# Output projection's weights loaded head group by head group, with a new recorded order, in a fused attention and MLP block

## The chip, the cores and the metric

The kernel runs on one core of one Trainium2 chip. The metric is device time in microseconds (us), the median of the runs; the kernel before was run three times. Beside these there is one profiled execution, of which every engine's instructions, the DMA queues and the semaphores are recorded. A core has five instruction streams: TensorE (PE for matmuls, PEld for the loads of their stationary operand), VectorE (DVE), ScalarE (ACT), GpSimd (POOL) and SyncE (SP), which here issues all DMAs. Each stream runs strictly in the order in which it was written.

## The reference

Inputs are bf16: 2048 rows of 576 numbers, 32 heads of 18, an MLP of 4608. Cut to what matters:

```python
def _A_ref(x, wq, wk, wv, wo, beta):          # x: layernorm of the input
    q, k, v = split_heads(x @ wq), split_heads(x @ wk), split_heads(x @ wv)
    ...
    for s in range(4):                        # four segments of 512 rows
        logits = einsum('bhqd,bhkd->bhqk', qs, ks) * scale + mask
        a_dot = einsum('bhqk,bhkd->bhqd', softmax(logits), vs)
        a_mem = (phi(qs) @ M) / (phi(qs) @ z + 1e-06)
        outs.append(g * a_mem + (1.0 - g) * a_dot)
        M, z = M + phi(ks).T @ vs, z + phi(ks).sum()
    return merge_heads(outs) @ wo
def _B_ref(x, w1, b1, w2, b2):
    return gelu(x @ w1 + b1) @ w2 + b2
h = x + _A_ref(layernorm(x), ...)
return h + _B_ref(layernorm(h), ...)
```

## The kernel before

**Tiling.** The 2048 rows are 16 tiles `t` of 128 rows, in 8 chunks `c` of 256. The steps of a tile have names, which the text uses:

- `x_p` (line 262) loads a tile of x; `bnp`, `aggrp`, `powp`, `nmrp`, `applyp`, `againp` (lines 363 to 383) are its layernorm; `PTx` (393) turns it on PE, with the copy `PTcx` (396) to SBUF, or `Tx` (154) turns it with a transposing DMA.
- `proj` (351, 355) multiplies with wq, wk, wv. The last 64 of the 576 rows of the weights are done for two products side by side in half the array each (`prest`, 427), or, for those listed in the table `WHOLE`, with a full-height matmul of their own. `pev` (482 to 491) takes the result from PSUM to SBUF. `PTq`, `PTk` (507) with `PTcq`, `PTck` (510, 511), or the transposing DMAs `Tq`, `Tk` (154), turn queries and keys into QT and KT.
- `score` (599): 16 small matmuls into one PSUM tile of four banks, `exp` (603) on ACT, `mask` (607) on POOL, `value` (615) back on PE. There are 80 such visits, and all use the same four banks: `score` v+1 cannot start before `exp` v is done. Two to four visits make one group of heads; `f_T`, `f_rec`, `f_gate`, `f_mul` (630 to 642) divide and gate the sum.
- The memory of earlier segments: `k_exp`, `k_relu`, `k_min`, `k_add`, `MZ`, `MZadd`, `MZblk` (520 to 549), and for the queries `m_exp` to `m_mul` and `mem` (561 to 577). The gate is made once by `g_exp`, `g_add`, `g_rec`, `g_omg`, `g_gmz` (337 to 345).
- `oT` (650) turns the attention's output, `wo` (659) multiplies with the output projection's weights, `res` (662) adds x, `bnb` to `againb` (675 to 695) are the second layernorm.
- `F1q` and `F1` (351, 355, with `rest`, 726, for the last 64 rows of w1) are the first layer of the MLP, `F1e` (745 on ACT, 747 on DVE) adds the bias, `gelu` (768) runs on ACT, `F2` (828) is the second layer, `ot` (834) adds the residual, which comes back from DRAM by `hc` (819).

**Order.** The functions only record operations with what they read and write. What runs, and where, is in five tables written out by hand of a search: `ORDER` (line 874) lists the operations as they are issued, one list for all engines; `FLIP` names those that go to their other engine (ACT instead of DVE, DVE instead of POOL, and so on); `WHOLE` is named above; `PLACE` gives each PSUM result its bank. Banks 0 to 3 are free for any use; banks 4 to 7 are the tile of the scores, or four more single banks (`st` in the profile) while no scores are in them. So a PSUM bank that is written anew waits for whoever still reads it.

**DMAs.** SP issues all of them in the order of `ORDER`. Eight semaphores are handed out in turn, so an issue also waits until the DMA eight issues before it has landed. A waiting issue holds back everything behind it.

**Output weights.** `wo_t` (128 partitions x 5 blocks x 576) holds the 576 rows of wo rearranged: partition 32i+p of block b has row 144i+32b+p, for the four groups i of 144 rows (8 heads each). Block 4 has 16 rows per group.

**Warm-up.** 37 matmuls on zeros (`zeros`, 334) stand between the first real PE work; they need `pq`, which the memset `pq0` (293) clears.

Of the kernel before, what the change touches and what calls it, by code (L numbers as in the profile page):

```python
# [16 lines left out]
def kernel(  # L17
# [15 lines left out]
    nc = tc.nc  # L33
    P = 128
    x = A_x.flatten_outer_dims()
    of = out.flatten_outer_dims()
    S, D = x.shape
# [8 lines left out]
    KT = 5  # L46
    HALF = D // 2
    G = H // 4
    R = D // 4
# [15 lines left out]
    def sbuf(name, shape, dt=BF16):  # L65
# [29 lines left out]
    }  # L95
    FLIP = {
# [8 lines left out]
    }  # L105
    WHOLE = {
        204, 397, 407, 417, 424, 487, 488, 561, 645, 792, 870, 871, 1103, 1519, 1840, 2159, 2160,
# [40 lines left out]
    def dma(name, kb, desc, issue, rd=(), wr=(), after=()):  # L148
        o = op(name, "SP", issue, rd, wr, after=after)
        o.kb, o.desc = kb, desc  # L150
        return o
# [7 lines left out]
    wo_t = sbuf("wo_t", [KT, D])  # L159
# [119 lines left out]
    rows_of = A_wo.rearrange("(i r) n -> i r n", r=R)  # L279

    def last_wo():
        nc.sync.dma_start(out=wo_t[0:96, 4, :], in_=A_wo[P:P + 3 * R, :].rearrange("(i r) n -> i r n", r=R)[:, 0:32, :])
        nc.sync.dma_start(out=wo_t[96:112, 4, :], in_=A_wo[D - 16:D, :])

    memset("wo0", "POOL", wo_t[96:P, 4, :], 0.0, [("wo", 4)])
    for b in range(4):
        kb = 180 if b < 3 else 144
        dma(("wo", b), kb, kb // 18, lambda b=b: nc.sync.dma_start(out=wo_t[:, b, :], in_=rows_of[:, 32 * b:32 * b + 32, :]), (), [("wo", b)])
    dma(("wo", 4), 18, 1, last_wo, (), [("wo", 4)])
# [565 lines left out]
    for c in range(NCH):  # L855
# [193 lines left out]
```

## Time and profile before

| | |
|---|---|
| three runs, us | 459.26, 459.88, 460.39; median 459.88 |
| the profiled execution's own time | 461.19 us |
| its span, from the first to the last instruction | 459.5 us |
| busy in the span: DVE, ACT, POOL | 270.4 us (59%), 327.1 us (71%), 232.6 us (51%) |
| read from HBM, written | 60.09 MB, 7.08 MB |
| mean granted TensorE clock | 0.996 of full speed |

A line of the profile's timeline has the start, the busy time, engine, source line, operation, `out<-in`, shapes and count; in square brackets is the engine's idle time before it and what ended it. "PEclk" is the share of the full TensorE clock that was granted. Busy time of PE counts a matmul until its modelled end, and consecutive ones overlap. "issue" means that an engine stood still although the profile shows nothing that it waited for. The lines themselves are shown in the prediction, where they are used.

### The profile page before, as it was taken

Reading aid. Unit: us, or ns where it says so; the run is one execution under the profiler, and the core shown is the slowest. Engines: PE = TensorE matmul, PEld = TensorE weight load, DVE = VectorE, ACT = ScalarE, POOL = GpSimd, SP = SyncE. Lnnn points to the kernel's source line nnn. Section 1 sums busy time; section 2 is a strip of 40 time slices with the busy share of each in tenths; the row PEclk is TensorE's granted clock in tenths of the full one; section 3 lists DMA queues with packets and bytes.
Section 4 is the critical chain, followed back from the end, with each engine's and each line's share of the span. In section 5 each row is a group of like instructions: output and inputs, shape, how many; then the busy total and the mean of one; then the engine's idle time right before and its main releaser. Section 6 shows DMA issues by size and latency. Waiting matters only on the chain.

```text
span 459.5 us, 14513 instructions
## 1 busy us (share of the span) xinstructions
PE 448.6 (98%) x6110; PEld 335.6 (73%) x6110; DVE 270.4 (59%) x616; ACT 327.1 (71%) x317; POOL 232.6 (51%) x419
## 2 busy tenths in 40 slices
PE   8899989999999999999999999999999999999997
PEld 6555868677667777766777767777777888888886
DVE  6697978878676676686757586752425432112221
ACT  5688879988878897878778879798967155453430
POOL 7677858687976557756462697654025002000000
PEclk9899999999999999999999999999999999999999
DMA  8589988554569675879545885676558647655212
GB/s 233 148 220 258 250 158 235 185 129 102 147 167 225 162 173 161 211 165 203 145 126 163 190 200 127 183 218 186 147 156 189 195 123 198 205 175 172 88 41 66
DMA packets 113253, 78.42 MB, mean 171 GB/s; under 512 B 47731, under 2 KB 111139, under 8 KB 113187
## 3 DMA queue, kind: packets, MB, share of 16 engines
q1 hardware_dynamic: 113187, 77.48, 65.3%
q8 instruction: 48, 0.79, 0.8%
q14 instruction: 18, 0.15, 0.1%
HBM read 60.09 MB, written 7.08 MB: 146 GB/s over the span
## 4 chain that ended last, share of the span: by engine, by line
PE 87%; DMA 5%; SPq 2%; issue 1%; DVE 1%; ACT 1%; POOL 1%; ACTq 0%; DVEq 0%
PE bank L351 27%; PE bank L828 24%; PE st L351 9%; PE st L828 6%; PE st L599 5%; PE bank L615 4%; PE bank L659 3%; PE bank L726 3%; PE bank L355 2%; DMA xT<-xn 1%; PE bank L569 1%; DMA x_p<-in_A_x_dram 1%; DMA x_b<-in_A_x_dram 1%; DMA w1g<-in_B_w_dram 1%; PE st L726 1%
## 5 line engine op out<-in xcount | busy, mean ns | idle before, releaser
L603 ACT ACTIVATE pt<-st 128x2048 bf16<-128x2048 f32 x80 | 150.1, 1877 | 43.8 <-PE st L599 34.2
L828 PEld LDWEIGHTS <-hT 128*128 128x128 bf16 x1188 | 111.4, 98 | 28.0 <-issue 1.2
L828 PE MATMUL bank<-w_sb,hT 128*128 128x288 bf16 (+1 forms) x936 | 131.3, 284 | 0.0
L607 POOL TENSOR_SCALAR_AFFINE_SELECT pt<-pt 128x512 bf16<-128x512 bf16 x128 | 80.0, 641 | 42.7 <-ACT pt L603 40.9
L351 PEld LDWEIGHTS <-w1g 128*128 128x128 bf16 x944 | 86.5, 98 | 18.4 <-issue 7.2
L351 PE MATMUL bank<-xn2T,w1g 128*128 128x256 bf16 (+1 forms) x760 | 93.7, 269 | 0.0
L747 DVE TENSOR_TENSOR hT<-bank,b1T 128x512 bf16<-128x512 f32 x77 | 52.0, 684 | 66.8 <-PE bank L351 63.0
L768 ACT ACTIVATE hT<-hT 128x1536 bf16<-128x1536 bf16 (+4 forms) x25 | 66.2, 2662 | 6.2 <-DVE hT L747 5.9
L745 ACT ACTIVATE hT<-bank,b1T 128x256 bf16<-128x256 f32 x66 | 27.5, 472 | 33.2 <-PE bank L351 32.9
L351 PE MATMUL bank<-wqkv,xT 128*128 128x432 bf16 (+1 forms) x208 | 45.4, 348 | 1.9 <-DVE QT L510 1.9
L351 PEld LDWEIGHTS <-xT 128*128 128x128 bf16 x264 | 24.4, 99 | 20.3 <-issue 4.9
L599 PE MATMUL st<-QT,KT 32*128 32x128 bf16 x1280 | 32.8, 218 | 2.4 <-issue 2.4
L834 DVE TENSOR_TENSOR ot<-bank,hc 128x288 bf16<-128x288 f32 (+1 forms) x26 | 11.6, 447 | 38.6 <-PE bank L828 25.6
L828 PE MATMUL st<-w_sb,hT 128*128 128x288 bf16 (+1 forms) x252 | 34.1, 277 | 0.0
L599 PEld LDWEIGHTS <-KT 32*128 32x128 bf16 x1280 | 18.7, 93 | 18.8 <-issue 16.0
L630 DVE STREAM_TRANSPOSE bank<-bank 128x512 f32<-128x512 f32 x32 | 23.2, 724 | 9.0 <-PE bank L615 8.7
L564 POOL TENSOR_TENSOR pq<-ek,pq 128x512 bf16<-128x512 bf16 x24 | 27.7, 1154 | 1.4 <-DVE ek L563 1.1
L351 PE MATMUL st<-xn2T,w1g 128*128 128x256 bf16 x184 | 24.7, 273 | 0.0
L643 POOL TENSOR_TENSOR o_nat<-t,t 128x288 bf16<-128x288 f32 x24 | 19.4, 808 | 9.7 <-DVE t L642 6.9
L667 POOL TENSOR_TENSOR h_t<-h_t,b_bc 128x576 f32<-128x576 f32 x16 | 20.6, 1284 | 6.6 <-DVE xn L685 6.6
L615 PE MATMUL bank<-pt,v_aug 128*19 128x128 bf16 x1280 | 23.6, 220 | 0.0
L615 PEld LDWEIGHTS <-v_aug 128*19 128x19 bf16 x1280 | 17.9, 92 | 5.7 <-issue 3.7
(159 smaller groups left out, 639.7 us busy)
## 6 DMA issues: line engine op xcount, KB each, us to landing
w1g<-in_B_w_dram SPq DMA_DIRECT2D x57, 512.0 KB, 4.2
w_sb<-in_B_w_dram SPq DMA_DIRECT2D x12, 432.0 KB, 5.5
wqkv<-in_B_w_dram SPq DMA_DIRECT2D x10, 512.0 KB, 4.6
hd<-h_t SPq DMA_DIRECT2D x16, 288.0 KB, 3.7
hc<-hd SPq DMA_DIRECT2D x32, 144.0 KB, 3.7
w1g<-in_B_w_dram SPq DMA_DIRECT2D x114, 32.0 KB, 3.2
x_b<-in_A_x_dram SPq DMA_DIRECT2D x18, 144.0 KB, 4.1
hT<-in_B_w_dram SPq DMA_DIRECT2D x5, 512.0 KB
```

The costliest lines, as they stand in the source:

```text
L351: nc.tensor.matmul(out=acc, lhsT=lhsT_of(slice(0, P), k), rhs=rhs_of(slice(0, P), k), start=start and k == 0, stop=False, skip_group_check ...
L564: op(("m_add", n), "POOL", lambda: nc.gpsimd.tensor_tensor(out=pq[:], in0=e_g, in1=pq[:], op=ALU.add), ["ek"], ["pq"])
L599: nc.tensor.matmul(out=st4[:, i, n * P:(n + 1) * P], lhsT=KTs[(2 * s0 + kt) % NK][rows, g, :], rhs=QTs[(2 * c + qt) % NQ][rows, g, :], sta ...
L603: op(("exp", v), "ACT", lambda pt=pt: nc.scalar.activation(out=pt[:], in_=open_four("scores")[:], func=ACT.Exp, scale=scale), [st], [("pt" ...
L607: op(("mask", v), "POOL", lambda n=n, pt=pt: nc.gpsimd.affine_select(out=pt[:, :, n * P:(n + 1) * P], in_=pt[:, :, n * P:(n + 1) * P], pat ...
L615: nc.tensor.matmul(out=bank(ox)[32 * i:32 * i + E, (g % 4) * P:(g % 4) * P + P], lhsT=v_augs[(2 * s0 + kt) % NV][:, G * i + g, :], rhs=pt[ ...
L630: op(("f_T", n), "DVE", lambda: nc.vector.transpose(out=bank(ox), in_=bank(ox)), [], [ox])
L667: op(("hb", t), "POOL", lambda: nc.gpsimd.tensor_tensor(out=h_t[:], in0=h_t[:], in1=b2_bc[:], op=ALU.add), ["b2"], hk)
L745: nc.scalar.activation(out=dst[:, j, :], in_=acc()[:, j, :], func=ACT.Identity, bias=b1T[:, j0 + j:j0 + j + 1], scale=1.0)
L747: op(name, "DVE", lambda: nc.vector.tensor_tensor(out=dst, in0=acc(), in1=bias, op=ALU.add), [tok, "b1T"], keys, alt=("ACT", by_act), afte ...
L768: op(("gelu", c, f0, f), "ACT", lambda: nc.scalar.activation(out=hT[:, f0:f, :], in_=hT[:, f0:f, :], func=ACT.Gelu_apprx_tanh), [], [("hT" ...
L828: nc.tensor.matmul(out=bank(b)[:, 0:w], lhsT=hT[:, q, tl * P:(tl + 1) * P], rhs=w2_sb[:, q, hs], start=(q == 0), stop=(q == NF - 1))
```

## The change

The load of wo is cut the other way. Before, block b was one DMA over all four groups: source rows as (4 groups) x (32 rows) x 576, 128 partitions; block 4 took a DMA for three groups (3 x 32 x 576) and one for the last 16 rows, six DMAs in all. After, group i is one DMA: source as (32 rows) x (5 blocks, 4 for the last group) x 576, into its 32 partitions, and one for the last 16 rows, five DMAs. The bytes are the same to within the rows of block 4 (for groups 0 to 2, block 4 takes 32 rows in both).

All five tables are new. The operations, their number and what they compute are the same. By the new tables:

- `WHOLE` has 16 entries instead of 17: the pair `rest` of chunk 1's first F1 products is now done in halves, three `prest` entries changed places;
- from DVE to ACT: 8 more `applyp` and 2 more `applyb`; from ACT to DVE: 6 `pev` and 2 `PTcx`; between DVE and POOL, 2 `againb` and 1 `againp` go to DVE, and some memsets change engine;
- DVE begins with the memset of MZacc ahead of `pq0` (before: `pq0` first);
- in the list of SP, `x_p` of tile 5 is the 16th DMA, and the loads of wo come right behind it (before: the three loads of blocks 1 and 4 come ahead of it, with that of b1 between); the first load of w2 stands 45th (before: 19th), the first of w1 21st (before: 29th);
- `Tk` of tile 4 is issued after score 8 (before: after score 14), `Tk` of tile 3 after score 7 (before: 11), `Tx` of tile 5 after score 5 (before: 6);
- `b1Tc` has `MZadd`, `MZadd`, `pev` ahead of it on DVE (before: `k_min`, `g_omg`, `g_omg`, `pev`, `aggrp`).

```diff
     PLACE = {
-        0: 0, 1: 1, 2: 2, 3: 3, 4: 0, 5: 4, 6: 3, 7: 1, 8: 4, 9: 0, 10: 2, 11: 0, 12: 5, 13: 2, 14: 2, 15: 1, 16: 4,
...
+        0: 0, 1: 1, 2: 2, 3: 3, 4: 3, 5: 2, 6: 3, 7: 3, 8: 5, 9: 2, 10: 0, 11: 5, 12: 4, 13: 1, 14: 4, 15: 3, 16: 6,
...
-    rows_of = A_wo.rearrange("(i r) n -> i r n", r=R)
-
-    def last_wo():
-        nc.sync.dma_start(out=wo_t[0:96, 4, :], in_=A_wo[P:P + 3 * R, :].rearrange("(i r) n -> i r n", r=R)[:, 0:32, :])
-        nc.sync.dma_start(out=wo_t[96:112, 4, :], in_=A_wo[D - 16:D, :])
-
     memset("wo0", "POOL", wo_t[96:P, 4, :], 0.0, [("wo", 4)])
-    for b in range(4):
-        kb = 180 if b < 3 else 144
-        dma(("wo", b), kb, kb // 18, lambda b=b: nc.sync.dma_start(out=wo_t[:, b, :], in_=rows_of[:, 32 * b:32 * b + 32, :]), (), [("wo", b)])
-    dma(("wo", 4), 18, 1, last_wo, (), [("wo", 4)])
+
+    for i in range(4):
+        n = KT if i < 3 else 4
+        rows = A_wo[i * R:i * R + 32 * n, :].rearrange("(b r) n -> r b n", r=32)
+        dma(("wo", i), 36 * n, 2 * n, lambda i=i, n=n, rows=rows: nc.sync.dma_start(out=wo_t[32 * i:32 * i + 32, 0:n, :], in_=rows), (), [("wo", i)])
+    dma(("wo", 4), 18, 1, lambda: nc.sync.dma_start(out=wo_t[96:112, 4, :], in_=A_wo[D - 16:D, :]), (), [("wo", 4)])
...
     ORDER = [
-        21, 64, 35, 53, 37, 27, 65, 55, 0, 66, 41, 67, 1, 68, 69, 70, 56, 57, 26, 10, 71, 72, 31, 51, 73, 22, 74, 75,
...
+        22, 55, 21, 20, 65, 49, 0, 53, 10, 1, 54, 56, 23, 66, 30, 2, 67, 57, 36, 68, 69, 70, 58, 5, 3, 71, 28, 143,
...
```

More of the change, by code (lines that the diff above doesn't have):

```diff
@@ L68 @@
     PLACE = {
[26 rows of a table removed]
[26 rows of a table added]
     }
     FLIP = {
[8 rows of a table removed]
[7 rows of a table added]
     }
     WHOLE = {
-        204, 397, 407, 417, 424, 487, 488, 561, 645, 792, 870, 871, 1103, 1519, 1840, 2159, 2160,
+        264, 397, 407, 417, 424, 487, 488, 561, 792, 793, 871, 1103, 1104, 1519, 2159, 2160,
     }
```

337 rows, old and new, of tables (FLIP, ORDER, PLACE) are left out of this document.

## The prediction

> **What bounds the kernel now.** I read the page first, then the sums by stretch, PE's waits, and the chain of the first 75 us.
>
> ```profile
> span 459.5 us, 14513 instructions
> ...
> PE 448.6 (98%) x6110; PEld 335.6 (73%) x6110; DVE 270.4 (59%) x616; ACT 327.1 (71%) x317; POOL 232.6 (51%) x419
> ...
> q8 instruction: 48, 0.79, 0.8%
> ```
>
> PE is busy 98% of the span. So the time is PE's own work plus the stretches in which it stands still or runs slowly.
>
> ```profile
> 14.61:18.02 3.41, 1.52 (x26) 0.83 (x15) 1.09 (x3) 2.43 (x3) 3.10 (x8) 1.00 0.50 152
> 18.02:21.44 3.42, 3.40 (x30) 1.94 (x30) 3.17 (x7) 0.77 (x2) 2.05 (x5) 0.50 0.51 126
> ...
> 60.00:70.00 10.00, 7.96 (x177) 6.76 (x174) 7.55 (x18) 7.13 (x6) 5.76 (x9) 1.00 0.76 136
> 70.00:260.00 190.00, 190.00 (x2834) 137.24 (x2832) 136.84 (x309) 159.81 (x139) 126.79 (x215) 1.00 0.67 170
> ...
> 270.00:350.00 80.00, 80.00 (x1126) 61.03 (x1127) 41.41 (x95) 65.54 (x60) 39.39 (x69) 1.00 0.66 171
> ...
> 360.00:450.00 90.00, 90.00 (x804) 73.31 (x802) 23.08 (x44) 35.72 (x50) 3.74 (x6) 1.00 0.50 147
> ```
>
> Columns: stretch and length, busy time (count) of PE, PEld, DVE, ACT, POOL, granted clock, DMA share, GB/s. From 70 to 450 us PE is full in all but two short stretches; nothing can be won there except by less work. The losses lie before 70 us: standing still, and one stretch of 3.42 us at half clock right behind a stretch in which PE was busy only 1.52 of 3.41.
>
> ```profile
> PE st L599 <- issue: 2.4, 2, 2.0
> PE bank L351 <- DVE QT L510: 1.9, 1, 1.9
> PE bank L334 <- DVE pq L293: 1.2, 1, 1.2
> PE bank L427 <- DMA xT<-xn: 1.1, 1, 1.1
> PE bank L427 <- DVE b1T L847: 0.9, 1, 0.9
> PE bank L726 <- DVE ot L834: 0.3, 1, 0.3
> PE bank L726 <- DMA w1g<-in_B_w_dram: 0.2, 1, 0.2
> ```
>
> These are all of PE's waits: 8.0 us, 1.2 of them the start. With the half clock (3.4 us for 1.7 us of work) 9.7 us are not full-speed work, and 8.0 of those lie between 15 and 64 us. That is the most that an order with the same work can win there.
>
> **PE's work does not change.** Operations and counts are the same but for `WHOLE`: one `rest` fewer there, so two matmuls of 256 columns less.
>
> ```profile
> 263.98 0.87 PE bank L351 x8
> ...
> 52.95 0.22 PE L355 MATMUL bank<-xn2T,w1g 128*128 128x128 bf16 x1
> 53.10 0.40 PE L599 MATMUL st<-QT,KT 32*128 32x128 bf16 x16
> ```
>
> Eight such matmuls take 0.87 us, so two give 0.2 us back. What an order could change besides is the switching between full-height matmuls and those in parts of the array: a score begins 0.15 us after the matmul of 128 columns ahead of it, which by the first row's rate (0.109 for 256) needs 0.055, so a switch costs about 0.1 us. Counted along PE's list there are 265 switches in both orders: no difference. ACT's changes between exp and gelu are also 22 in both. So everything hangs on the waits.
>
> **The wait at 16 us and the half clock: -1.9 and -1.7.**
>
> The first fence has issues from SP's timeline, SP's waits, and the landing times of line 262; the second the chain and DVE's timeline.
>
> ```profile
> 9.46 0.67 SPq L288 DMA_DIRECT2D wo_t<-in_A_wo_dram  x1
> ...
> 11.94 0.36 SPq L262 DMA_DIRECT2D x_p<-in_A_x_dram  x1
> ...
> 14.80 2.69 SPq L705 DMA_DIRECT2D w1g<-in_B_w_dram  x3
> ...
> SPq L705 <- DMA wo_t<-in_A_wo_dram: 1.8, 2, 1.0
> ...
> DMA to landing us min/median/max: 2.2/4.1/7.0
> ```
> ```profile
> 11.94 4.97 DMA x_p<-in_A_x_dram
> ...
> 16.93 0.46 DVE L363 BATCH_NORM_STATS2 stats_p<-x_p 128x6 f32<-128x288 bf16 x1 [2.54 <-DMA x_p<-in_A_x_dram]
> 17.31 0.67 DVE L510 COPY QT<-bank 128x1024 bf16<-128x1024 bf16 x1
> ```
>
> Tile 5's x is issued at 11.94, behind three loads of wo, and takes 4.97 us; the loads of line 262 take 2.2 at best, 4.1 in the median. DVE meets its `bnp` and stands 2.54 us. Behind it in DVE's list is the copy of QT, which frees a PSUM bank, and PE waits 1.9 us for that. In the changed list this load is the 16th DMA, ahead of wo's, and `bnp` of tile 5 stands later in DVE's list, behind `pev` of tile 1. As the 16th it leaves SP at about 10.2 us (the 16th of before did, 0.7 after the one shown at 9.46), and with the median of 4.1 it lands at 14.3. On PE 12.7 us of work stand ahead of the end of the product that this `pev` reads, which with a start at 1.8 (below) is 14.5; so DVE comes to `bnp` at about 15 and finds its data. I take the whole 1.9 (bounds 0, if the load again takes 4.97 and more, and -1.9). The slow stretch goes with it: -1.7 (bounds 0 and -1.7).
>
> The new cut of wo matters for what is queued behind. Rows: two issues waited 1.8 us for wo's loads; the first, issued at 9.46, had not landed before 14.80, 5.3 us for 180 KB, where 144 KB of x took 2.2. The Trainium skill, "DMA: Bandwidth & Descriptors", section "Why a DMA increments its semaphore by 16 and not by 1", says that a copy goes over as many engines, 16 at most, as divide the slowest dimension of both sides: that would be 4 before and 16 after. Were it so, the 1.8 us of SP would go; were the slowness only general traffic, they would stay, and up to 1.8 us of waits for the transposing DMA of tile 3 with them. No view here shows the engines of one DMA. I add neither to the sum; 1.8 goes into the range.
>
> **Two more waits, -0.9 and -1.1.**
>
> ```profile
> DMA to landing us min/median/max: 2.6/4.3/9.0
> ...
> 25.16 1.34 DVE L341 TENSOR_SCALAR omg<-g_bc 32x8 f32<-32x8 f32 x2
> ...
> 27.27 0.14 DVE L847 CAST b1T<-bank 128x36 f32<-128x36 bf16 x1
> ...
> 35.12 6.08 DMA xT<-xn
> ```
>
> `b1Tc`, 0.14 us of work, is late because two tiny `g_omg` (32x8) took 1.34 us ahead of it. The new DVE list has `MZadd` and `pev` there, of 0.4 to 0.6 us each, and on PE `proj` of tile 3 and a `value`, about 1 us, come between the b1 transpose and the next use of the bank. I take -0.9 (bounds 0, -0.9). `Tx` of tile 5 took 6.08 us at 35.12, behind 432 KB of w2; in the new list no load of w2 is ahead of it, and 5.5 us of PE work lie between the last use of its buffer and its first reader (before: 5.8). The transposing DMAs of line 154 take 4.3 us in the median (the first row), which fits into 5.5. I take -1.1 (bounds 0, -1.1).
>
> **The two "issue" waits, 2.4: -1.2.**
>
> ```profile
> 50.48:63.13 12.65, 10.61 (x256) 9.49 (x256) 11.39 (x25) 9.23 (x7) 9.89 (x18) 1.00 1.03 236
> ```
>
> Between the two PE does exactly 256 matmuls and 256 weight loads. The page's instruction queue moved 48 packets, 0.79 MB: 16 KB each, for PE's 12,220 instructions 255 apiece. So these look like waits for instructions, at every second boundary, in a stretch where the DMA engines are full (share 1.03). Of some 47 boundaries two are late. Which ones will be after depends on what the DMA engines carry then; the new list has no transposing DMA between score 8 and score 14, but as much weight data. I take half, -1.2 (bounds 0, -2.4).
>
> **What is given back: +0.4 and +0.5.**
>
> ```profile
> 1.28 0.56 DVE L258 MEMSET MZacc<- 128x608 f32 x1
> ```
>
> This memset now precedes `pq0`, so PE starts 0.56 us later; part of that falls into the slow clock of the start. I take +0.4 (bounds +0.3, +0.6). For new waits I counted, for each PE operation of both lists, PE's work between it and the PE operation on which it hangs through another engine. Most kinds of such pairs agree: between one score and the next the least is 2.16 us (before 2.04), with 22 of 79 under 2.4 (before 23). Somewhat tighter are F2 to the reuse of its bank through `ot` (0.87, before 1.32) and F1 through a DVE `F1e` (1.30, before 1.41). I allow +0.5 for new waits (bounds 0, +4: ten waits like the 0.2 to 0.4 us on line 726).
>
> **The sum** on the profiled execution: -1.9 -1.7 -0.9 -1.1 -1.2 -0.2 +0.4 +0.5 = -6.1. Its span 459.5 becomes 453.4, its own time 461.2 becomes 455.1. The median of the runs is 1.3 lower, 459.9; I carry the difference over: **453.8**.
>
> **Rivals.**
> *The clock.* The slow stretch is exactly as long as the one before it, and starts where that ends: the clock seems set in fixed stretches of 3.41 us by how busy PE was in the last one (1.52 of 3.41). A wait of 1.9 us that falls across two stretches would then cost no clock; the 2.0 us wait at 61 did not, the clock of 60 to 70 being 1.00. If the wait at 16 us fell across two in the timed runs, they had no slow stretch, and the gain is 6.1 - 1.7: 455.5. For it: the timed runs are 1.3 under the profiled one; against: nothing else in the profile. "TensorE: Matmul & The Clock Gate" in the Trainium skill, section "What's actually happening", states that the window runs freely and does not start anew with the kernel; the trace's 3.41 us agrees with the length that it gives, and one profile cannot show the rest.
> *Only the 16 us wait goes.* DMA waits return under other names, since the bytes are the same: -1.9 -1.7 -0.2 +0.4 = -3.4, 456.5. For it: the DMA share of 1.03; against: in the new list the transposing DMAs come earlier, relative to their readers.
> *Nothing is gained.* The new waits (+4 at the bound) and the unchanged ones take back the sum: about 459.9.
> *Slower: ACT holds the scores.*
>
> ```profile
> L603 ACT ACTIVATE pt<-st 128x2048 bf16<-128x2048 f32 x80 | 150.1, 1877 | 43.8 <-PE st L599 34.2
> ...
> L378 ACT ACTIVATE xn<-x_p,nmr_p,rstd_p 128x576 bf16<-128x576 bf16 x2 | 1.7, 857 | 0.0
> ...
> L482 ACT CAST qk_pad<-bank 128x432 bf16<-128x432 f32 x8 | 4.1, 517 | 1.9 <-PE bank L355 1.0 <-PE bank L351 0.9
> ...
> 80.00:90.00 10.00, 10.00 (x162) 7.07 (x161) 9.08 (x21) 9.83 (x8) 5.61 (x12) 1.00 0.67 213
> ```
>
> Ten more `apply` of 0.86 us go to ACT, which is busy 9.83 of 10 us at 80 to 90. If each falls between two exps and holds the next score by all of it, PE loses 8.6 us and the time is 462.4; from 0.61 us each the whole gain is gone, from 0.75 the kernel is slower. Against: six `pev` (0.52 each) leave ACT; the 80 exps found ACT idle 43.8 us, 0.55 each, mostly waiting for PE; and in PE's waits none names ACT.
>
> **Chances.** Forecast 0.58 (its own range 451.5 to 456); clock 0.12; only the first wait 0.12; nothing gained 0.06; ACT 0.12. Lowest, all of the 8.0 is won and 0.2 of work, less 0.3 at the start: 452.0; the 0.5 of PE's late waits and the 0.6 by which the fastest run lies under the median bring it to 450.9. Upwards I reach past the second rival by the 1.8 of SP, to 458.3; this leaves out the last two. About 0.3% is what a measurement of this kernel can tell from no change: faster 0.58 + 0.12 + 0.12 = 0.82, same 0.06, slower 0.12.
>
> **What would show it.** Right: no DVE wait for `x_p` near 16 us and no PE wait on QT; granted clock 1.00 from 5 us on; no wait on `b1T` or on a transposed xT in PE's list; PE's waits under 4.5 us in all, start included. Wrong: PE's waits again near 8 us before 70 us; a PE wait on ACT, or exps that start later than 0.4 us behind their score; many short waits on `ot` or `hT` behind 70 us; PE's first matmul near 1.2 us rather than 1.8.

## The result, and the profile after

| | before | after |
|---|---|---|
| median, us (4 runs each) | 460.13 (459.26 to 460.85) | 455.71 (453.71 to 456.73) |
| profiled execution's own time, span | 461.19, 459.5 | 456.73, 455.0 |

The ratio of the runs is 0.9899 (95% interval 0.9857 to 0.9942): the change takes off about 1%, 4.4 us of the 6.1 that were forecast. The time lies inside the range, 1.9 above the forecast.

The page of the changed kernel:

```profile
span 455.0 us, 14518 instructions
...
PE 447.2 (98%) x6110; PEld 335.0 (74%) x6110; DVE 269.6 (59%) x618; ACT 331.7 (73%) x322; POOL 229.7 (50%) x412
...
L598 ACT ACTIVATE pt<-st 128x2048 bf16<-128x2048 f32 x80 | 150.1, 1877 | 40.5 <-PE st L594 33.2
```

The bound is the same, PE at 98%, and the exps find ACT nearly as idle as before (40.5 us, was 43.8). All of PE's waits:

```profile
PE bank L329 <- DVE MZacc L257: 1.9, 1, 1.9
PE bank L346 <- DMA w1g<-in_B_w_dram: 1.8, 1, 1.8
PE bank L350 <- DMA hT<-in_B_w_dram: 1.1, 1, 1.1
PE bank L721 <- DVE ot L829: 0.2, 1, 0.2
```

The copy of QT, b1T, the transposed xT and both waits by the name of issue are gone. In their place stand two waits for w1 (the last rows of w1 lie in `hT`), and the start is longer. They add to 5.0 us, where the forecast had named less than 4.5 as a sign that it was right.

The sums by stretch of the changed kernel, and one row of before for comparison:

```profile
5.50:7.40 1.90, 1.90 (x10) 1.31 (x9) 1.83 (x7) 1.17 (x3) 0.80 (x2) 1.00 0.83 189
...
18.00:21.50 3.50, 3.50 (x47) 2.20 (x44) 3.00 (x11) 3.29 (x4) 2.98 (x9) 1.00 0.28 57
...
30.00:70.00 40.00, 37.06 (x797) 28.76 (x796) 33.12 (x74) 35.72 (x33) 29.89 (x55) 1.00 0.91 226
...
70.00:260.00 190.00, 189.90 (x2807) 136.03 (x2806) 135.60 (x308) 162.37 (x145) 129.70 (x220) 1.00 0.72 175
```
```profile
5.50:7.40 1.90, 1.90 (x25) 1.74 (x23) 1.79 (x7) 0.69 (x1) 0.97 (x3) 1.00 1.04 287
```

At 18 us PE is full and its clock whole: the half-clock stretch is gone. Behind 70 us PE is as full as before. But in the 1.9 us from 5.5 the new kernel's PE does 10 matmuls where before did 25: here its clock is still slow, as it is at the start of every profile. From start to start a warm-up matmul of 256 columns takes 0.213 us until 7.46 us, and 0.109 from then on; in before the step came at 4.37. (The column of the granted clock shows 1.00 in both rows; it says nothing of this first stretch. The count of matmuls does, and by it the forecast's sign of a full clock from 5 us on is not met.)

Where x of tile 5 was late, in the DVE and SP timelines of the changed kernel:

```profile
10.80 0.33 SPq L261 DMA_DIRECT2D x_p<-in_A_x_dram  x1
```
```profile
17.12 0.46 DVE L358 BATCH_NORM_STATS2 stats_p<-x_p 128x6 f32<-128x288 bf16 x1
...
19.41 0.64 DVE L505 COPY QT<-bank 128x1024 bf16<-128x1024 bf16 x1
```

The load left SP at 10.80 us and took 4.1, so it landed at 14.9, and no idle time stands in brackets at `bnp` (17.12). And the two new waits, PE first, then SP:

```profile
50.37 0.22 PE L350 MATMUL bank<-xn2T,hT 128*128 128x128 bf16 x1 [1.08 <-DMA hT<-in_B_w_dram]
...
67.65 0.61 PE L346 MATMUL bank<-xn2T,w1g 128*128 128x256 bf16 x4 [1.81 <-DMA w1g<-in_B_w_dram]
```
```profile
41.60 4.32 SPq L153 DMA_TRANSPOSE KT<-qk_pad  x1
45.97 0.58 SPq L700 DMA_DIRECT2D hT<-in_B_w_dram  x1
...
58.67 2.24 SPq L153 DMA_TRANSPOSE xT<-xn  x1
60.96 0.59 SPq L700 DMA_DIRECT2D w1g<-in_B_w_dram  x1
62.01 0.94 SPq L697 DMA_DIRECT2D w1g<-in_B_w_dram  x2
```

Both loads leave SP behind a transposing DMA: the last rows of w1 of slot 2 behind `Tk` of tile 4, whose issue alone took 4.32 us, and w1 of slot 5 behind `Tx` of tile 6. Slot 5's load could have left at 56.9, when PE had read its buffer; it left at 62.01.

### The profile page after: what moved, and what is told of

Its sections match the earlier page's. It is cut to its first block, busy times and chain, and to the rows that moved or that the text cites. A ratio compares the mean times of both kernels' runs of the same rounds, so it can differ in the third digit from the quotient of the medians.

```text
span 455.0 us, 14518 instructions
## 1 busy us (share of the span) xinstructions
PE 447.2 (98%) x6110; PEld 335.0 (74%) x6110; DVE 269.6 (59%) x618; ACT 331.7 (73%) x322; POOL 229.7 (50%) x412
## 4 chain that ended last, share of the span: by engine, by line
PE 89%; DMA 4%; DVE 2%; SPq 1%; ACT 1%; issue 1%; POOL 1%; DVEq 0%; POOLq 0%; ACTq 0%
PE bank L346 27%; PE bank L823 24%; PE st L346 9%; PE st L823 6%; PE st L594 5%; PE bank L610 4%; PE bank L654 3%; PE bank L721 3%; DMA w1g<-in_B_w_dram 2%; PE bank L329 2%; PE bank L350 1%; PE st L721 1%; PE bank L564 1%; DMA hT<-in_B_w_dram 1%; DMA hc<-hd 1%
## 5 line engine op out<-in xcount | busy, mean ns | idle before, releaser
L598 ACT ACTIVATE pt<-st 128x2048 bf16<-128x2048 f32 x80 | 150.1, 1877 | 40.5 <-PE st L594 33.2
L346 PE MATMUL bank<-xn2T,w1g 128*128 128x256 bf16 (+1 forms) x776 | 96.2, 269 | 1.9 <-DMA w1g<-in_B_w_dram 1.8
L740 ACT ACTIVATE hT<-bank,b1T 128x256 bf16<-128x256 f32 x70 | 29.0, 472 | 32.4 <-PE bank L346 32.2
L346 PE MATMUL bank<-wqkv,xT 128*128 128x432 bf16 (+1 forms) x196 | 41.6, 342 | 0.0
L346 PE MATMUL st<-xn2T,w1g 128*128 128x256 bf16 x168 | 23.2, 273 | 0.0
```

The costliest lines, as they stand in the source:

```text
L346: nc.tensor.matmul(out=acc, lhsT=lhsT_of(slice(0, P), k), rhs=rhs_of(slice(0, P), k), start=start and k == 0, stop=False, skip_group_check ...
L598: op(("exp", v), "ACT", lambda pt=pt: nc.scalar.activation(out=pt[:], in_=open_four("scores")[:], func=ACT.Exp, scale=scale), [st], [("pt" ...
L740: nc.scalar.activation(out=dst[:, j, :], in_=acc()[:, j, :], func=ACT.Identity, bias=b1T[:, j0 + j:j0 + j + 1], scale=1.0)
```

## The experiments

Before ran again beside each group of kernels, on the same chip, with medians of 460.58 (the first four below), 461.38 (the loads of w1, both edits, w2 and `Tk`) and 460.51 (the rest); ratios are against these. The profiles also serve a question of their own, the clock at the start, at the end of this section. An edit of the order is written as pairs (n, m): operation n is moved to right ahead of m.

### Is it the place of tile 5's load, or the cut of wo?

Before, with x of tile 5 (551) ahead of the first load of wo (15):

```diff
     ]
+    for n, m in ((551, 15),):
+        ORDER.remove(n)
+        ORDER.insert(ORDER.index(m), n)
```

> The kernel before with one edit: x of tile 5 is issued ahead of the first load of wo instead of behind three of them. If the place in SP's list is the cause of the 1.9 us wait (theory), tile 5's x leaves at about 9.5 us and lands by 14, its bnp on DVE finds its data, PE does not wait on the copy of QT, the granted clock stays 1.00 around 18 us, and 1.9 + 1.7 = 3.6 us go: about 456.4. If it is the cut of wo (rival), the loads of wo still hold their part of the engines and the wait passes to the next load that DVE or PE needs: within 1 us of before, 459 to 460.

459.05 (10 runs), ratio 0.9961 (0.9932 to 0.9990). DVE in this kernel:

```profile
14.79 0.44 DVE L363 BATCH_NORM_STATS2 stats_p<-x_p 128x6 f32<-128x288 bf16 x1
15.15 0.67 DVE L510 COPY QT<-bank 128x1024 bf16<-128x1024 bf16 x1
```

PE's waits, the largest behind the start and issue:

```profile
PE bank L659 <- DMA wo_t<-in_A_wo_dram: 0.8, 1, 0.8
PE bank L427 <- DVE v_aug L486: 0.8, 1, 0.8
PE bank L427 <- DMA xT<-xn: 0.6, 1, 0.6
PE bank L427 <- DVE b1T L847: 0.5, 1, 0.5
```

The mechanism is as the theory has it: data there, copy of QT at 15.15 instead of 17.31, no wait of PE on it, no slow stretch. But the gain is half of the 3.6 or less, and the time lies in the range of the rival. Two things take from it. Waits of 0.8 for wo and for a `pev` come up. And in most executions there was no slow stretch to win: each run has its mean granted clock on record, and one stretch of 3.41 us at half clock lowers it to 0.996. Of the 27 runs of before beside this group nine have 0.996 or 0.993, the others 0.999 or 1.000. Of the ten runs of this kernel none is under 0.999.

Before, with the new cut of wo alone (the lines of the change that load wo, nothing else):

```diff
-    for b in range(4):
-        kb = 180 if b < 3 else 144
-        dma(("wo", b), kb, kb // 18, lambda b=b: nc.sync.dma_start(out=wo_t[:, b, :], in_=rows_of[:, 32 * b:32 * b + 32, :]), (), [("wo", b)])
...
+    for i in range(4):
+        n = KT if i < 3 else 4
+        rows = A_wo[i * R:i * R + 32 * n, :].rearrange("(b r) n -> r b n", r=32)
...
```

> The kernel before with the new cut of wo's loads alone; all five tables are the old ones (the operation of the last rows is one DMA instead of two). Theory (place in the list): x of tile 5 still leaves behind three loads of wo, DVE still stands over 1.5 us, PE over 1 us at 16 us and half the clock behind it; 459 to 460.5. Rival (the cut): the loads of wo land in 4 to 5 us instead of 5 to 8, x of tile 5 lands within 3.5 us instead of 4.97, before 15.5, PE's wait at 16 us falls under 0.6 and the slow stretch goes: 456 to 457.5.

458.67 (10 runs), ratio 0.9969 (0.9939 to 0.9999), between the times of the two. The theory does not hold: the wait on QT is gone here too, with the old place in the list. DMA issues of the first 40 us in this kernel, median us to landing last, and one row of before:

```profile
x_p<-in_A_x_dram SPq DMA_DIRECT2D x6, 144.0 KB, 3.7
wo_t<-in_A_wo_dram SPq DMA_DIRECT2D x3, 180.0 KB, 4.7
```
```profile
x_p<-in_A_x_dram SPq DMA_DIRECT2D x6, 144.0 KB, 5.6
```

Ahead of x of tile 5 SP issues two loads of wo, in 0.33 and 0.38 us, where before it issued three, in 0.67, 0.80 and 0.38. So this x leaves at 10.72 instead of 11.94. It lands 3.7 us later, at 14.4, instead of 4.97 later, at 16.9. DVE then:

```profile
13.97 0.46 DVE L480 CAST qk_pad<-st 128x288 bf16<-128x288 f32 x1 [1.22 <-PE st L351]
...
15.66 0.44 DVE L359 BATCH_NORM_STATS2 stats_p<-x_p 128x6 f32<-128x288 bf16 x1
16.03 0.67 DVE L506 COPY QT<-bank 128x1024 bf16<-128x1024 bf16 x1
```

No idle time stands at `bnp` (15.66). DVE is about 1.2 us late here because it waited 1.22 us for PE, whose slow warm-up lasted until 6.86 us in this execution, not 4.37. In before DVE was free for `bnp` at 14.39 (16.93 less 2.54), about when x lands here; the copy of QT would then end near 15.4 (17.31 less 2.54, and 0.67 of work), and PE was not ready for it before 16.1 (18.04 less the wait of 1.91). So by this estimate, which rests on one profile of each, the cut alone takes the whole wait, and the different warm-up had no part in it. A half-clock stretch can still come: three of the ten runs have a mean granted clock of 0.996, and the profile has such a stretch behind a stall of 2.9 us at 59 to 61 us, which is used below.

The changed kernel with the old cut, its tables kept (the same lines the other way round):

> The changed kernel with the old cut of wo's loads (six DMAs), its own five tables kept. Theory (the order does it): within 0.7 us of the changed kernel's 455.7, with PE waits in the same places. Rival (the cut does it): the loads issued behind wo's at 11 to 13 us come later by 1 to 2 us, and PE waits 1 us or more before 30 us with a slow clock behind it: 457.5 or more.

457.20 (10 runs), ratio 0.9926 (0.9901 to 0.9952): between the two. The wait is the rival's, but no slow clock followed it. PE's timeline:

```profile
24.48 0.91 PE L350 MATMUL bank<-wqkv,xT 128*128 128x432 bf16 x4 [1.40 <-DMA xT<-xn]
26.41 0.46 PE L536 MATMUL bank<-v_aug,phik_pad 128*128 128x76 bf16 x8 [0.54 <-DVE v_aug L488]
```

`Tx` of tile 3 leaves SP at 20.48 instead of 18.80, and PE waits for it. So the order alone is worth 0.74%, the cut alone 0.31%, and both 1.01%: two parts that add, as far as these intervals tell, of which the forecast counted one. The intervals are wide: this kernel is not told apart from the changed one (0.9899, 0.9857 to 0.9942).

### The start

The changed kernel with `pq0` (21) ahead of the memset of MZacc (55):

```diff
+    for n, m in ((21, 55),):
```

> The changed kernel with pq0 ahead of the memset of MZacc on DVE, as it was before. PE's first matmul moves from 1.88 to 1.2-1.3 us in either case. In the changed kernel's profile the warm-up matmuls of 256 columns took 0.213 us each until 7.45, in that of before until 4.38. If the end of that slow stretch hangs on the start of PE's work alone (locked to the kernel), it ends near 4.4 again, and 0.64 + 1.1 us go: about 454.0. If its end is drawn from stretches of 3.41 us that run freely, the end in this profile is anywhere between about 3.5 and 7.9 us, unlike both, and the median moves by about 0.3 to 0.6 us only: 455.1 to 455.4.

455.31 (6 runs), ratio 0.9903 (0.9875 to 0.9931). First matmul at 1.24, the end of the slow warm-up at 6.04: neither 4.4 nor 7.45. The second theory holds. What the edit is worth cannot be told: the median is 0.4 under the 455.71, the ratio is not lower.

### The two loads of w1

The changed kernel with w1 of slot 5 (364) ahead of its last rows (366), and the last rows of slot 2 (120) ahead of `Tk` of tile 3 (276):

```diff
+    for n, m in ((364, 366), (120, 276)):
```

> The changed kernel with two loads moved up in SP's list: w1 of slot 5 ahead of its last rows, a load of w2 and Tx of tile 6 (it was issued at 62.01 and landed at 67.60, 1.89 us late for PE), and the last rows of w1 of slot 2 ahead of Tk of tiles 3 and 4 (issued at 45.97 behind 3.04 and 4.32 us of issuing, landed at 50.23, 1.24 late). Theory (each is late by its place behind the transposing DMAs): neither wait is left, 3.1 us go, about 452.6. Rival (the DMA engines are full from 40 to 66 us, so the wait only changes its name): PE's waits between 35 and 70 us stay above 1.5 us in all, 454 to 455.7.

454.17 (4 runs), ratio 0.9853 (0.9807 to 0.9899): the time that the rival gave. Both waits are gone, as the theory had it; of 30 to 70 us PE is busy 39.37 instead of 37.06:

```profile
30.00:70.00 40.00, 39.37 (x821) 30.70 (x821) 35.34 (x79) 36.13 (x32) 30.91 (x59) 1.00 0.93 232
```

In the profile that is 2.3 of the 3.1; by the ratios (0.9853 against 0.9899) about 2, but their intervals overlap. What these waits are worth, the changed kernel itself shows, run once more:

> The changed kernel once more, unchanged, beside the next run on the same chip. Theory (the TensorE clock is granted in stretches of 3.41 us that run freely, and DMA landings differ from run to run): the first matmul again at 1.88 us, the warm-up slow until another time than 7.45, anywhere between 5.0 and 8.0; PE's waits for w1 near 49 and 66 us again, over 2 us together, give or take 1. Rival (the profile of one run is the kernel): 7.45 within 0.1, and the same waits within 0.1. Median 455 to 457.

455.48 (6 runs), ratio 0.9894 (0.9870 to 0.9917). Its PE waits, all of them, and the sums by stretch that show its warm-up and where the wait lies:

```profile
PE bank L329 <- DVE MZacc L257: 1.9, 1, 1.9
PE bank L346 <- issue: 0.7, 1, 0.7
```
```profile
5.50:7.40 1.90, 1.90 (x14) 1.51 (x13) 1.73 (x7) 1.17 (x3) 0.98 (x3) 1.00 0.84 159
...
0.00:56.94 56.94, 54.27 (x861) 37.28 (x862) 49.09 (x126) 49.24 (x58) 43.86 (x105) 1.00 0.83 210
```

The expectation of over 2 us for w1 missed: in this execution SP came to slot 5 at 59.6, not 62.01, and PE waited for w1 under 0.3 us. So the two waits belong to some executions and not to the kernel. Four profiles have these loads in their old places: the first one of the changed kernel, this one, that with `pq0` first and that with the old cut. The wait of 1.8 for slot 5 stands in the first alone, the wait for the last rows of slot 2 in the first (1.1) and with `pq0` first (0.3). A profile without them, as that with the loads moved up, therefore does not show that the move took them away.

Both edits together:

```diff
+    for n, m in ((21, 55), (364, 366), (120, 276)):
```

> The two loads moved up as in the run before, and pq0 ahead of the memset of MZacc. If the two edits add (theory): the 3.1 of the loads and the 0.4 by which pq0 first lowered the median, about 452.2. PE's first matmul at 1.24, the end of the slow warm-up anywhere between 4.3 and 7 us. Rival as there: 454 to 455.5.

455.19 (4 runs), ratio 0.9868 (0.9824 to 0.9912). No wait for w1, but one of 0.8 by the name of issue: not the 452.2 of the theory but the rival's time, and not told apart from either edit alone.

With four loads of w2 (139 to 142) later, ahead of x of tile 10 (1432):

```diff
+    for n, m in ((21, 55), (364, 366), (120, 276), (139, 1432), (140, 1432), (141, 1432), (142, 1432)):
```

> As the run before, and four of the seven loads of w2 (432 KB each) that stand between 37 and 58 us go behind the last load of w2, at about 79 us; their first readers start at 92 us. If the bytes that are not needed yet are what makes the waits between 30 and 66 us (theory of full engines), all waits in that stretch go, those for instructions too, and it is 0.5 to 2 us faster than the run before: 450.5 to 452. If they were late by place alone, it is the same as the run before within 0.4, or loses up to 2 us where F2 waits for w2 at 92 to 95 us.

456.92 (6 runs), ratio 0.9896 (0.9857 to 0.9935): if anything slower than without, where the theory of full engines had 450.5 to 452. That theory is not borne out. F2 did not wait for w2. What was late is x of tile 10, in SP's and DVE's timelines:

```profile
76.59 4.85 SPq L845 DMA_DIRECT2D w_sb<-in_B_w_dram  x6
81.54 2.75 SPq L261 DMA_DIRECT2D x_p<-in_A_x_dram  x1
```
```profile
90.99 0.46 DVE L358 BATCH_NORM_STATS2 stats_p<-x_p 128x6 f32<-128x288 bf16 x1 [2.35 <-DMA x_p<-in_A_x_dram]
...
91.73 0.30 DVE L484 CAST v_aug<-bank 128x144 bf16<-128x144 f32 x1
```

This is the wait of before at 16 us, made anew: an x behind several large loads, `bnp` standing at the head of DVE, and behind it a `pev` for which PE waits 1.6 us.

### The waits by the name of issue

Before, with `Tk` of tile 5 (572) and of tile 4 (499) moved 29 and 10 us down SP's list:

```diff
+    for n, m in ((499, 791), (572, 432)):
```

> The kernel before with Tk of tile 5 (issued at 45.68, 4.1 us long) moved to 75 us and Tk of tile 4 (issued at 54.99, 5.7 us long) to 65 us; the issue waits of PE were at 50.1 and 61.1, each behind one of the two. If PE's instructions come late because the queues are held up by these transposing DMAs (theory), neither wait is there and PE has none by the name of issue before 65 us: 2.4 to 2.8 us go, about 457.5, unless one comes up behind the new places. If it is the plain load of the engines (rival), the two waits stay, over 1.5 us in all, near the same instructions: 460.

460.30 (10 runs), ratio 0.9988 (0.9955 to 1.0020): no difference that can be told, though the waits of this name fell from 2.4 to 0.2 us. The profile has other waits in their place, 0.6 and 0.5 us on DVE among them. In the four other profiles of before's order the waits of this name add to 0.9 to 3.3 us. So the 0.2 of one profile points to the transposing DMAs, but does not prove it, and what the move is worth is not shown.

Before, with 26 warm-up matmuls of 256 columns made as two of 128:

```diff
-        op(("zeros", z), "PE", lambda w=w, n=n: nc.tensor.matmul(out=bank(w)[:, 0:n], lhsT=pq[:, 0, :], rhs=flat[:, 0:n], start=True, stop=True),
-           ["pq"], [w])
+        def zeros(w=w, n=n, step=n if z < 11 else P):
+            for c in range(0, n, step):
+                nc.tensor.matmul(out=bank(w)[:, c:c + step], lhsT=pq[:, 0, :], rhs=flat[:, c:c + step], start=True, stop=True)
+        op(("zeros", z), "PE", zeros, ["pq"], [w])
```

> The kernel before with its last 26 warm-up matmuls of 256 columns each made as two of 128: 26 matmuls and 26 weight loads more, the same time for PE. In before, the two issue waits stood at the 608th and the 864th matmul, 256 matmuls apart. If they are PE waiting for the next block of its instructions (theory), they stand at the same counts from the start again, so at operations 26 matmuls earlier in the program (about 1.5 us earlier at the same work), and the second is as long or longer. If they belong to the operation (rival: an unseen wait of that score or F1q), they stand at the same operations, the 634th and the 890th matmul.

One run, 456.95, too few to read a time from. PE's timeline and the count of matmuls ahead of it, then the same of before:

```profile
48.27 0.46 PE L617 MATMUL bank<-pt,v_aug 128*19 128x128 bf16 x19 [0.87 <-issue]
...
0.00:48.26 48.26, 43.33 (x607) 27.96 (x607) 39.73 (x106) 37.20 (x48) 37.22 (x91) 1.00 0.86 218
```
```profile
50.49 0.34 PE L599 MATMUL st<-QT,KT 32*128 32x128 bf16 x9 [0.37 <-issue]
63.14 0.23 PE L599 MATMUL st<-QT,KT 32*128 32x128 bf16 x3 [2.04 <-issue]
...
0.00:50.48 50.48, 44.91 (x607) 28.43 (x607) 40.10 (x107) 37.33 (x48) 37.31 (x91) 0.97 0.86 216
```

The first wait came at the 608th matmul again, now in a `value` and no longer in a score: it belongs to the count. The second, at the 864th, did not come. In the other kernels the issue waits of this stretch lie at the same count to within two, whatever the operation: behind 861 matmuls in the changed kernel's second profile above, 861 with `pq0` first, 862 with the new cut in before. With the packets of some 255 instructions that the prediction read from the page, the likely cause is that PE waits for its next block of instructions there; no view shows the block itself arrive. Which boundary is late differs from run to run.

### A version that beats both

The changed kernel with all that held: `pq0` first, the two loads of w1 up, x_b of tile 1 (305) ahead of two loads of w1, and the four loads of w2 behind x of tile 10, not ahead of it:

```diff
+    for n, m in ((21, 55), (364, 366), (120, 276), (305, 125), (139, 406), (140, 406), (141, 406), (142, 406)):
```

> The changed kernel with the two loads moved up and pq0 first, x_b of tile 1 ahead of two loads of w1 (it was issued behind them and landed 7.8 us later, for a wait of 0.3 to 1.1 us at 44 us), and the four loads of w2 not at 37 to 48 us but right behind x_p of tile 10, at 82 us, so that no x waits behind them as in the run in which they stood ahead of it (9.4 us to land, 1.78 us for PE). Theory: no wait over 0.3 us is left before 100 us beside the start; 1.2 us under the run with pq0 and the two loads: 453.3 to 454.2. Rival (w2 comes too late for F2 at 92 to 95 us, or the bytes hold up others there): a wait of 1 us or more behind 85 us, 455 or more.

453.26 (451.86 to 454.20, 5 runs), ratio 0.9848 (0.9818 to 0.9878). The second runs of the changed kernel, on the same chip, lie from 455.29 to 456.05: all above these. The theory's time and waits came, about 2.2 us under the changed kernel. It has four edits at once, and which of them does it is not shown; the profiled execution, 451.86, is the fastest of the five. Its only PE wait, and its stretches:

```profile
PE bank L329 <- DVE pq L288: 1.2, 1, 1.2
```
```profile
30.00:70.00 40.00, 40.00 (x815) 31.10 (x814) 36.41 (x82) 37.23 (x30) 30.95 (x60) 1.00 0.86 190
70.00:260.00 190.00, 190.00 (x2805) 136.37 (x2804) 134.29 (x307) 163.97 (x149) 130.97 (x219) 1.00 0.77 186
```

### The clock, from all the profiles

The end of the slow warm-up in the profiles, from the step in the time between matmuls (us):

| first matmul | end of the slow stretch, one profile each |
|---|---|
| 1.24 | 4.37 (before), 4.89, 4.92, 5.35, 5.40, 5.72, 6.04, 6.48, 6.86 |
| 1.88 | 6.51, 6.64, 7.34, 7.46 (after) |

The same start is followed by ends 2.5 us apart, and the changed kernel, profiled twice, has 7.46 and 6.64. So the end does not hang on the start alone: the stretches of 3.41 us run freely, as the clock rival had it. The Trainium skill, "TensorE: Matmul & The Clock Gate", section "What's actually happening", states that the window is free-running and does not reset when a kernel starts; this table agrees. Once the phase is known, later stretches follow: before's slow stretch starts at 4.37 + 4 x 3.413 = 18.02. In the kernel with the new cut alone, 6.86 + 16 x 3.413 = 61.46; in that with `Tk` moved, 5.72 + 4 x 3.413 = 19.37. The third fence is from the first profile of the changed kernel, whose stretches begin at 7.46; 7.46 + 17 x 3.413 = 65.48:

```profile
58.05:61.47 3.42, 0.79 (x21) 0.51 (x18) 2.77 (x7) 0.96 (x2) 2.22 (x5) 1.00 1.00 88
61.47:64.88 3.41, 3.13 (x31) 2.93 (x32) 0.69 (x1) 1.88 (x1) 1.37 (x2) 0.50 0.51 149
```
```profile
15.96:19.37 3.41, 1.73 (x11) 0.81 (x10) 1.94 (x6) 1.83 (x2) 3.20 (x9) 1.00 0.39 115
19.37:22.78 3.41, 2.90 (x39) 1.83 (x38) 3.33 (x8) 3.05 (x3) 1.65 (x3) 1.00 0.52 110
```
```profile
65.49:68.90 3.41, 1.60 (x43) 1.31 (x28) 2.00 (x6) 3.38 (x3) 1.50 (x2) 1.00 1.04 342
68.90:72.31 3.41, 3.41 (x39) 2.76 (x36) 2.18 (x5) 3.41 (x1) 1.61 (x5) 1.00 1.20 217
```

The first: PE busy 0.79 of 3.42, then half the clock. The second has the same wait on QT as before (1.7 us), busy 1.73 of 3.41, and the clock stays whole; in before it was 1.52, and fell. The third holds the new wait of 1.8 us for w1, busy 1.60, and the clock stays whole there too. The wait alone does not bring the slow stretch; how much of one stretch it leaves PE busy does.

How often it came, the runs tell. Of the 53 runs of before beside the three groups, 20 have a mean granted clock of 0.993 to 0.996, one or two such stretches, and a median of 462.30. The other 33 have 0.999 or 1.000, and a median of 459.87. All ten runs of the changed kernel have 1.000. The record does not say where in a run the stretch stood.

## Why the prediction was right, and where it was wrong

| term of the sum | forecast | in the two profiles |
|---|---|---|
| wait on the copy of QT | -1.9 | -1.9 |
| half clock behind it | -1.7 | -1.7 |
| b1T | -0.9 | -0.9 |
| transposed xT of tile 5 | -1.1 | -1.1 |
| the two issue waits | -1.2 | -2.4 |
| work | -0.2 | not read singly |
| start | +0.4 | +0.6 and +1.1 |
| new waits | +0.5 | +2.6 |

The terms with a number add to -3.7; the span fell by 4.5. The 0.8 left are `WHOLE`'s 0.2 and small steps, none of which I can name. The +2.6 is 1.8 + 1.1 + 0.2 less the 0.3 and 0.2 that before had on line 726. The +1.1 is 11 warm-up matmuls at 0.213 instead of 0.109 us.

*Direction and mechanism were right.* The waits that the order was to remove are gone, each where the prediction placed it, and the slow stretch with the first. The other profiles bear it out. A wait on b1T (0.5 to 1.1 us) stands in all five profiles of before's order and in none of the eight of the changed one. Without the start, PE's waits add to 3.7 to 6.8 us in the five, and to 0 to 4.0 in the eight. Rival "only the first wait goes" is out: b1T, the transposed xT and the issue waits went too. "Nothing is gained" is out by the interval.

*The wait at 16 us: right in size, one cause of two.* The place in the list was taken as the cause and the cut put at nothing. The two runs on before show that the place alone removes the wait, and that the cut alone does so too; the changed kernel with the old cut puts about 0.3% on the cut, within wide intervals. With the cut, x landed 2.5 us earlier, 1.2 of it by leaving SP earlier, which the prediction did not count, and 1.3 by a shorter flight. In the changed kernel x left SP at 10.80 and landed at 14.9, close to the forecast's 10.2 and 14.3; DVE came to `bnp` at 17.12 and not at 15. What the Trainium skill says in "DMA: Bandwidth & Descriptors", section "Why a DMA increments its semaphore by 16 and not by 1", that a copy goes over as many engines as divide the slowest dimension of both sides, pointed the right way. Loads of 180 KB landed in 4.7 us (the median of three) instead of the 5.3 that was read from one load of before. How many engines one DMA used, these views do not show.

*The half clock: right for the profile, not for the kernel.* That was the clock rival's point, and its mechanism is shown: in two other profiles of before's order with this wait (1.7 and 1.1 us) no slow stretch followed. The step that failed is the one that carried the -1.7 from the profiled execution over to the median of the runs. The 33 of 53 runs of before without a slow stretch have a median of 459.87, where the forecast started from 459.88: so the runs around the median most likely had no such stretch to lose. By the 20 of 53 the term was worth about 0.6 us in the mean, an estimate that takes every such stretch for this one, and next to nothing in the median. The sum without it is the clock rival's 455.5, and 455.71 was measured. That the two are so close is in part luck, since in the two profiles other terms of the sum were off by 1.2 to 2.1 us, in both directions.

*The start: mis-sized.* +0.4 took the later memset as all there was. The first 0.6 is as forecast; the rest was the warm-up's phase, and the profile of before had the shortest of all in the table above. With the same start it could have been up to 2.5 us longer, at half cost: an estimate of 1.2 us that the order does not decide. What the later memset costs in the median is not settled.

*New waits: the term that was most off in these two profiles.* They were priced at +0.5 by counting PE's work between dependent operations through other engines, and at most at ten short waits on DVE. What came were two loads of w1. The prediction had noted that "the new list has no transposing DMA between score 8 and score 14": it looked at what is no longer in that stretch, and not at which loads stand in SP's list behind the transposing DMAs. The two `Tk` at 38 to 46 us held SP for 3.0 and 4.3 us, with the DMA engines' share at 1.08 and 1.15. But +2.6 is the size of one execution: the three other profiles with these loads in the same places have 0, 0.3 and 0 of these two waits. So the list makes such waits possible, and in the median their worth stays open.

*Issue waits: right in kind, half the size.* Both went, not one. With 0 to 1.2 us of them in the other seven profiles of the changed order, and 0.2 to 3.3 in those of before's, "half" is fair for the kernel and low for this pair.

*ACT holds the scores: refuted.* No PE wait names ACT; ACT is 4.6 us busier, and its idle time ahead of the exps fell by 3.3 only.

## What to carry to other kernels

Where the bound engine is 98% busy, its few waits can be priced one by one, but price with each move what stands behind the moved operation in the queue that issues it; here two weight loads stood behind transposing DMAs, and came late in some executions. An input's small load belongs ahead of large loads that are needed later, above all when the operation that waits for it stands in an engine's queue ahead of work that the bound engine needs. And one profile is one draw: terms that hang on the clock's phase or on a DMA's landing should be counted by their chance, from several profiles, or for the clock from the granted clock of every timed run. A term of a profiled execution that the median run does not have must not be taken off the median.

## What the runs showed of the hardware that was not expected

The slow warm-up lasted 3.1 to 5.6 us after the first matmul, and 5.6 and 4.8 in two executions of the same kernel. Stretches of 3.41 us in which PE was busy 1.60 or 1.73 left the next at full clock, those with 1.52 and 0.79 did not. PE stood still at fixed counts (the 608th and about the 863rd matmul) for up to 2.9 us, in a stretch of short matmuls with full DMA engines (a share of 1.03 in before); these waits were at 0.2 in the one profile in which the transposing DMAs had been moved away. Cut the other way, with the same bytes, loads of wo took SP 0.33 to 0.56 us to issue (median 0.38), against 0.59 to 0.67 before.
